# Threshold attention with a gated feed-forward on one core: v in longer packets, part of the threshold subtraction on GpSimd, and a planner that models shared transfer engines

## The chip, the core and the metric

The kernel runs on one core of a Trainium2 chip. The core has five engines with queues of their own: TensorE (PE, matrix products; PEld is its weight load), VectorE (DVE), ScalarE (ACT), GpSimd (POOL) and SyncE (SP, which here only issues DMAs). The metric is the device time of one execution in microseconds, lower is better; the time before is a median of three runs.

## The reference

```python
# q, k, v: (8, 8, 576, 64) float32; tau = 0.02; moe_w_in (512, 2048), moe_w_out (2048, 512) float64
scores = matmul(q, k.transpose(0, 1, 3, 2)) / sqrt(64)
thresh = max(scores, axis=-1) - tau                  # per query row
scores = where(scores >= thresh, scores, -1e9)
attn   = exp(scores - max(scores)) ; attn /= sum(attn, -1) + 1e-9
x      = matmul(attn, v)  -> (8*576, 512)            # heads side by side
h      = x @ w_in
out    = (h * sigmoid(1.702 * h)) @ w_out
```

Softmax sums, maxima and products with v do not depend on the order of the 576 keys, as long as k and v are taken in the same order.

## The kernel before

**Units of work.** The 64 heads are taken as 32 pairs (two heads of one batch entry, `n` = 0 to 31); four pairs make the 576 rows of one batch entry, and the feed-forward takes rows in blocks of 256. In a pair the 576 keys are nine chunks of 64 (`j`), the queries two halves. Scores lie transposed in SBUF, two chunks to a tile: four full tiles of 128x1152 and a tail of 128x576 (`t` = 0 to 4).

**The steps of a pair.** `load_qk` brings q and k with SP's queue (32x18x32 elements to a DMA, four each), `prep` (L477, DVE) transposes them, `scores_run` (L493, PE) makes a chunk of scores, `keep` (L510, ACT) copies it to SBUF, `in_groups` (L516, DVE) takes maxima tile by tile. `over_tiles`, `over_halves` and `turn_rows` make one row of thresholds, which goes to DRAM and back with `row_out` and `row_in` (SP) to be spread over the partitions (pair 2 spreads it with `spread_max` on DVE). Then for each of the five tiles: `sub` (L580, DVE) subtracts the threshold, `mask` (L586, ACT) and `exps` (L590, ACT) make the weights, and PE multiplies by v (`values`, L601, out `pv`). The sums come from PE for pairs 0 to 4 (`sums_by_pe`, L601, out `den`, read by `one_row`, L632), from `in_groups` again for the others: pairs 5 to 7 spread them with `one_group` and `spread_sums` on DVE, pairs 8 to 31 with `turn_sums`, `sums_out`, `sums_in` through DRAM. `place_x` (L703, DVE) multiplies `pv` by the reciprocal sums into `xT`. `load_v` brings v with four DMAs, 64x9x64 elements each (every key's 64 numbers are a run of 256 bytes).

**The weights.** `w_in` and `w_out` arrive as 64-bit numbers in 32 pieces (16 and 16). `load_w` (POOL's queue, two DMAs of about 512 KB a piece) brings one; `cv_ex`, `cv_frac` (two instructions), `cv_end` (L439, L453, L457, L465, DVE) and `cv_power` (L447, ACT) make float32 of it. Six staging places hold pieces in flight. `hold` (L484, POOL) keeps the first pieces back until the k of pairs 2 and 3 has been transposed.

**The feed-forward.** The first two blocks (`mm1_0`, L758, 128 products of 128x256; `mm2`, L740) wait for `place_x` of pairs 0 to 3 and for pieces of `w_in` in groups of four. Later blocks use `mm1` (L718) and `product` (L909), the last four blocks `product1` (L823).

**The order.** Nothing is ordered at run time: each engine's queue is written out by a planner (`run_in_order`), which simulates tasks with a cost, a lag and a rank each, and lets each engine take the ready task of the lowest rank. Ranks are the pair's number plus a table of biases by step (`EARLY` for pairs 0 to 3, `SECOND` for 4 to 7, `LATER`, and `CV` for weights). In the kernel before a load is one task with a fixed cost on its queue and a fixed lag until it has landed (9.0 for a weight piece, 3.0 to 10.0 for q and k). Engine queues run in order, so that an instruction that waits holds back all behind it.

Of the kernel before, what the change touches and what calls it, by code (L numbers as in the profile page):

```python
# [19 lines left out]
P = 128  # L20
# [10 lines left out]
def kernel(  # L31
# [84 lines left out]
    stop = const.tile([P, 1], FP32, name="stop")  # L116
    shift = const.tile([P, 1], FP32, name="shift")
# [9 lines left out]
    for x in ("raw0", "raw1", "qkT0", "qkT1", "mb"):  # L127
# [6 lines left out]
        "exps": -11.47,  # L134
        "in_groups": 5.75,
        "keep": 10.66,
        "load_qk": -0.27,
        "load_v": 4.86,
        "mask": -2.66,
        "one_group": -15.86,  # L140
        "one_row": 12.67,
        "over_halves": -7.01,
        "over_tiles": -4.01,
        "place_x": -17.11,
        "prep": -11.73,
        "row_in": 20.49,
        "row_out": 4.47,
        "scores_run": 12.45,
        "spread_max": -1.73,
        "spread_sums": 7.14,  # L150
        "sub": 9.27,
        "sums_by_pe": 0.27,
        "sums_in": -9.39,
        "sums_out": 2.13,
        "turn_rows": -12.55,
        "turn_sums": -0.41,
        "values": 14.64,
        "w_sum": 4.11,
        "x_sum": -14.1,
    }  # L160
    SECOND = {
        "exps": -7.29,
        "in_groups": 20.95,
        "keep": 16.67,
        "load_qk": -8.88,
        "load_v": 5.53,
        "mask": 2.36,
        "one_group": 2.55,
        "one_row": -2.71,
        "over_halves": -12.07,  # L170
        "over_tiles": 2.86,
        "place_x": -20.26,
        "prep": 3.49,
        "row_in": -19.42,
        "row_out": -24.08,
        "scores_run": -7.99,
        "spread_max": -3.11,
        "spread_sums": -2.29,
        "sub": 14.98,
        "sums_by_pe": 35.93,  # L180
        "sums_in": 7.43,
        "sums_out": 4.05,
        "turn_rows": -3.84,
        "turn_sums": 4.03,
        "values": 11.79,
        "w_sum": -10.45,
        "x_sum": -10.98,
    }
    LATER = {
        "exps": 2.01,  # L190
        "in_groups": 10.37,
        "keep": -0.02,
        "load_qk": -6.6,
        "load_v": 3.77,
        "mask": 14.79,
        "one_group": 4.78,
        "one_row": -14.98,
        "over_halves": 1.09,
        "over_tiles": -6.27,
        "place_x": -0.34,  # L200
        "prep": 2.34,
        "row_in": 4.02,
        "row_out": 2.64,
        "scores_run": -11.25,
        "spread_max": -9.44,
        "spread_sums": -6.73,
        "sub": 2.14,
        "sums_by_pe": 1.46,
        "sums_in": 3.78,
        "sums_out": 2.16,  # L210
        "turn_rows": 12.26,
        "turn_sums": 0.29,
        "values": -10.38,
        "w_sum": 6.61,
        "x_sum": 6.02,
    }
    CV = {
        "cv_end": -8.05,
        "cv_ex": 2.22,
        "cv_frac": -11.72,  # L220
        "cv_power": -4.72,
        "load_w": -7.79,
    }

    LAG = {"PE": 0.26, "DVE": 0.18, "ACT": 0.22, "POOL": 0.18}

    QUARTERS = ("scores", "scores_run", "values", "sums_by_pe")
# [12 lines left out]
    FIRST, LAST = -9.0, 1000.0  # L240
    need, follows = {}, {}

    def run_in_order():
# [7 lines left out]
        events = [(0.0, 1, i) for i, n in enumerate(left) if n == 0]  # L251
# [3 lines left out]
        mode, held_for = None, None  # L255
        while events:
            now = events[0][0]
            while events and events[0][0] <= now:
                _, kind, i = heapq.heappop(events)
                engine, _, rank, _, _, _, _, give, lag = tasks[i]  # L260
                if kind == 0:
                    busy.discard(engine)
                    heapq.heappush(events, (now + lag, 2, i))
                elif kind == 1:
                    ready.setdefault(engine, []).append((rank, i))
                else:
                    for pool in give:
                        free[pool] += 1

                for u in users[i]:  # L270
                    if kind == (0 if tasks[u][0] == engine else 2):
                        left[u] -= 1
                        if left[u] == 0:
                            ready.setdefault(tasks[u][0], []).append((tasks[u][2], u))
            for engine, queue in ready.items():
                if engine in busy:
                    continue
                for rank, i in sorted(queue):
# [14 lines left out]
                cost = tasks[i][1]  # L293
                if engine == "PE":
# [3 lines left out]
                heapq.heappush(events, (now + cost, 0, i))  # L298
                started += 1
# [4 lines left out]
    JOINT = 7  # L304

# [53 lines left out]
    def load_qk(n, which, queue):  # L359
# [4 lines left out]
        for h in range(2):  # L364
            for j in range(2):
                queue.dma_start(
                    out=blocks[ds(64 * h + 32 * j, 32), :, :],
                    in_=src[b, 2 * hp + h, :, ts(j, 32)].rearrange("(c p) d -> p c d", p=32),
# [3 lines left out]
    def load_v(n):  # L372
        b, hp = divmod(n, NPAIR)
        t = seat("v_m", n % 2).rearrange("p (j h d) -> p j h d", j=NK, h=2)
        for h in range(2):
            for c in range(2):
                nc.sync.dma_start(
                    out=t[ts(c, KT), :, h, :],
                    in_=v[b, 2 * hp + h].rearrange("(j k) d -> k j d", k=KT),
# [109 lines left out]
    def scores(n, j):  # L489
# [8 lines left out]
        if j == NK - 1:  # L498
# [33 lines left out]
    def over_halves(n):  # L532
        r = stats[n, ALU.max]
        o = work.tile([P, QB], FP32, name="fold", tag="fold", bufs=1)
        for x in (1, 3) if n in BY_DMA else range(4):
# [3 lines left out]
            )  # L539
        if n in BY_DMA:  # L540
# [10 lines left out]
    def turn_rows(n):  # L551

        nc.vector.transpose(out=flat[1], in_=flat[0])

# [23 lines left out]
    def sub(n, t):  # L578
        s = sT[n, t].rearrange("p u h s -> p u (h s)")
        nc.vector.tensor_tensor(  # L580
# [26 lines left out]
    def values(n, tiles):  # L607
# [3 lines left out]
        by_values(n, lambda j, h: v_m[:, j, h, :], [pv[:, c, :] for c in range(2)], tiles)  # L611
        if n < NPAIR:
            free_scores(n, tiles)

    def sums_by_pe(n, tiles, apart):
# [9 lines left out]
        if not apart:  # L625
# [321 lines left out]
    nc.gpsimd.memset(ones, 1.0)  # L947
    nc.gpsimd.dma_start(
# [26 lines left out]
    BY_PE = 5  # L975
    BY_DMA = (0, 1, *range(3, NP))
    SUMS_BY_DMA = range(8, NP)
    LEAD = 6
    WHOLE = 6

    FFU = 1.727
    T_RANK = FIRST

    W_RANK = (0, 12.87, 12.51, 22.24, 0, 4.97)
    ready_w, w_loads, w64 = [], [], 0
    for i in range(len(pieces)):
# [10 lines left out]
        a = task("POOL", 1.1, rank, load_w, i, after=w_loads[-1:], take=place, lag=9.0)  # L997
        w_loads.append(a)
        e = task("DVE", 0.345, rank, cv_ex, i, after=[a])
        m = task("ACT", 0.67, rank, cv_power, i, after=[e])  # L1000
        a = task("DVE", 1.1, rank, cv_frac, i, after=[e])

        over = [ready_w[y] for y in range(i) if i >= n_in and stage(y) == (i - n_in) // PER_STAGE]
        ready_w.append(task("DVE", 0.61, rank, cv_end, i, after=[a, m] + over, give=place))
# [191 lines left out]
    for n in range(NP):  # L1196
# [5 lines left out]
        slow = 1.1 if n < NPAIR else 1.0  # L1202
# [3 lines left out]
        cost = 3.5 if NPAIR <= n < 2 * NPAIR else 2.0  # L1206
        lag = (4.6, 3.0)[n] if n < 2 else 10.0 if n < 2 * NPAIR else 3.0
        lq = task("SP", cost, r - 2.0, load_qk, n, 0, q0, after=behind, take=own(n, "raw0"), lag=lag)
        lk = task(
            "SP", cost if n else 0.1, r - 2.0, load_qk, n, 1, q1, after=behind,  # L1210
            take=own(n, "raw1"), lag=lag,
        )
        v_m = f"v_m{n % 2}"
        lv = task("SP", 2.4, r + (1.85 if n < 2 else -1.2), load_v, n, after=lvs[-1:], take=(v_m,), lag=3.0)
        lvs.append(lv)
        pq = task("DVE", 0.69, r, prep, n, 0, after=[lq], take=own(n, "qkT0"), give=own(n, "raw0"))
# [45 lines left out]
        else:  # L1262
            for js in [range(x, x + 3) for x in range(0, NK, 3)] if n >= WHOLE else [[x] for x in range(NK)]:
# [4 lines left out]
                    give=own(n, "qkT0", "qkT1") if js[-1] == NK - 1 else (),  # L1268
# [4 lines left out]
        a = task("DVE", 0.35, r, over_tiles, n, ALU.max, after=mx)  # L1273
        a = task(
            "DVE", 0.8 if n in BY_DMA else 1.05, r, over_halves, n, after=[a, tau_done],
# [100 lines left out]
```

## Time and profile before

| | |
|---|---|
| median of three runs | 1317.71 us (1317.33 to 1318.2) |
| profiled execution: time, span | 1317.94 us, 1316.2 us |
| mean granted TensorE clock | 0.987 |
| busy: PE, DVE, ACT, POOL | 1260.9, 1006.1, 646.6, 249.0 us |
| first matmul of the feed-forward (`mm1_0`) | 117.60 us after the span's start |

The profiled execution lasts 1.74 us longer than its span. PE's busy time and its idle time add up to the span, so that the kernel's time can be read as PE's work plus the gaps in PE's queue. Idle time of another engine counts only where it turns into such a gap.

### The profile page before, as it was taken

Reading aid. Unit: us, or ns where it says so; the run is one execution under the profiler, and the core shown is the slowest. Engines: PE = TensorE matmul, PEld = TensorE weight load, DVE = VectorE, ACT = ScalarE, POOL = GpSimd, SP = SyncE. Lnnn points to the kernel's source line nnn. Section 1 sums busy time; section 2 is a strip of 40 time slices with the busy share of each in tenths; the row PEclk is TensorE's granted clock in tenths of the full one; section 3 lists DMA queues with packets and bytes.
Section 4 is the critical chain, followed back from the end, with each engine's and each line's share of the span. In section 5 each row is a group of like instructions: output and inputs, shape, how many; then the busy total and the mean of one; then the engine's idle time right before and its main releaser. Section 6 shows DMA issues by size and latency. Waiting matters only on the chain. (4 is left out here: it accounts for less than half of the span.)

```text
span 1316.2 us, 22807 instructions
## 1 busy us (share of the span) xinstructions
PE 1260.9 (96%) x9128; PEld 975.6 (74%) x9128; DVE 1006.1 (76%) x1610; ACT 646.6 (49%) x830; POOL 249.0 (19%) x291
## 2 busy tenths in 40 slices
PE   5669999999999999999999999999999999999998
PEld 2346864457887777777778888777777778888887
DVE  7989999898888887788777877777888863652642
ACT  4876666576554555555554555454556540210210
POOL 1201211012031211213021303030212117120120
PEclk8879999999999999999999999999999999999999
DMA  8976766545323223212213222323122110000000
GB/s 152 293 189 207 230 207 149 112 77 100 85 55 71 55 55 71 51 50 54 58 42 72 55 71 55 71 55 71 36 55 54 36 46 8 9 1 25 8 0 32
DMA packets 258819, 102.88 MB, mean 78 GB/s; under 512 B 233754, under 2 KB 243994, under 8 KB 258714
## 3 DMA queue, kind: packets, MB, share of 16 engines
q1 hardware_dynamic: 244986, 63.40, 22.4%
q0 software_dynamic: 11360, 37.74, 9.3%
q8 instruction: 71, 1.16, 0.4%
q10 hardware_dynamic: 2368, 0.30, 0.2%
q14 instruction: 34, 0.28, 0.1%
HBM read 87.51 MB, written 9.69 MB: 74 GB/s over the span
## 5 line engine op out<-in xcount | busy, mean ns | idle before, releaser
L516 DVE TRANSPOSE_TENSOR_REDUCE part<-arena 128x36 f32<-128x1152 f32 (+1 forms) x295 | 357.5, 1235 | 41.9 <-ACT arena L510 32.4
L718 PE MATMUL hps<-xT,w_in 128*128 128x256 f32 x1536 | 337.2, 380 | 0.5 <-DVE arena L730 0.4
L718 PEld LDWEIGHTS hps<-xT,w_in 128*128 128x128 f32 x1536 | 290.7, 190 | 45.9 <-issue 5.7
L586 ACT ACTIVATE arena<-arena 128x1152 f32<-128x1152 f32 (+1 forms) x160 | 169.4, 1059 | 144.0 <-DVE arena L580 143.8
L510 ACT COPY arena<-ps 128x576 f32<-128x576 f32 x288 | 170.7, 647 | 115.3 <-PE ps L493 111.9
L580 DVE TENSOR_TENSOR arena<-arena 128x1152 f32<-128x1152 f32 (+1 forms) x158 | 201.1, 1313 | 20.5 <-DMA arena<-row 20.5
L909 PE MATMUL ops<-w_out,arena 128*128 128x256 f32 x896 | 202.4, 380 | 1.8 <-DVE arena L730 1.8
L590 ACT ACTIVATE arena<-arena,shift,scl 128x1152 f32<-128x1152 f32 (+1 forms) x160 | 200.3, 1252 | 4.1
L493 PE MATMUL ps<-arena 64*64 64x288 f32 x2304 | 174.7, 420 | 22.9 <-DVE arena L477 15.3
L909 PEld LDWEIGHTS ops<-w_out,arena 128*128 128x128 f32 x896 | 169.3, 190 | 28.7 <-DVE arena L730 3.1
L875 POOL TENSOR_TENSOR arena<-arena 128x256 f32<-128x256 f32 x56 | 49.7, 888 | 647.1 <-DVE arena L730 543.9
L601 PE MATMUL pv<-arena 64*64 64x288 f32 x2176 | 159.7, 408 | 0.0
L727 ACT ACTIVATE th<-hps 128x512 f32<-128x512 f32 x112 | 66.0, 589 | 186.0 <-PE hps L718 171.8
L909 PE MATMUL ops<-arena 128*128 128x256 f32 x672 | 150.7, 380 | 0.7 <-DVE osb L931 0.7
L493 PEld LDWEIGHTS ps<-arena 64*64 64x64 f32 x2304 | 84.0, 137 | 90.8 <-ACT arena L510 30.4
L909 PEld LDWEIGHTS ops<-arena 128*128 128x128 f32 x672 | 127.1, 190 | 20.4 <-issue 2.2
L601 PEld LDWEIGHTS pv<-arena 64*64 64x64 f32 x2176 | 82.1, 134 | 54.1 <-issue 10.0
L931 DVE SCALAR_TENSOR_TENSOR osb<-ops,osb 128x256 f32<-128x256 f32 x98 | 39.3, 413 | 97.9 <-PE ops L909 90.6
L730 DVE SCALAR_TENSOR_TENSOR arena<-th,hps 128x512 f32<-128x512 f32 x96 | 64.2, 669 | 46.7 <-ACT th L727 46.4
L740 PE MATMUL ops<-w_out,arena 128*128 128x512 f32 x128 | 57.2, 600 | 3.2 <-DVE w_out L465 2.2
L758 PE MATMUL hps<-xT,w_in 128*128 128x256 f32 x256 | 56.4, 381 | 0.0
L888 POOL TENSOR_TENSOR arena<-arena 128x512 f32<-128x512 f32 x28 | 35.6, 1272 | 108.3 <-PE ops L909 108.3
(115 smaller groups left out, 1044.7 us busy)
## 6 DMA issues: line engine op xcount, KB each, us to landing
arena<-in_v_dram SPq DMA_DIRECT2D x128, 144.0 KB
arena<-in_q_dram SPq DMA_DIRECT2D x128, 72.0 KB
out_dram<-osb SPq DMA_DIRECT2D x36, 256.0 KB
arena<-in_k_dram SPq DMA_DIRECT2D x124, 72.0 KB
arena<-row SPq DMA_DIRECT2D x62, 144.0 KB
arena<-row_s SPq DMA_DIRECT2D x48, 144.0 KB
w_out<-in_moe_w_in_dram POOLq DMA_DIRECT2D x12, 512.0 KB, 9.5
arena<-in_moe_w_out_dram POOLq DMA_DIRECT2D x12, 512.0 KB, 6.3
```

The lines of the kernel that those rows point to most:

```text
L493: nc.tensor.matmul(ps[ts(c, KT), h, 0:SH], lhsT=mats[n, 1][ts(h, D), ts(j, KT)], rhs=mats[n, 0][ts(h, D), ts(c, SH)], start=True, stop=True,)
L510: nc.scalar.copy(out=sT[n, t][:, u], in_=pss.pop((n, j))[:, :, 0:SH])
L516: nc.vector.tensor_reduce(out=stats[n, op][:, t * 2 * QB : min(2 * t + 2, NK) * QB], in_=sT[n, t].rearrange("p u h (g d) -> p (u h g) d", ...
L580: nc.vector.tensor_tensor(out=s, in0=s, in1=mbs[n].unsqueeze(1).to_broadcast(list(s.shape)), op=ALU.subtract)
L586: nc.scalar.activation(out=s, in_=s, func=AF.Prelu, alpha=STEEP)
L590: nc.scalar.activation(out=s, in_=s, func=AF.Exp, scale=scl, bias=shift)
L601: nc.tensor.matmul(o[c][ts(h, D), 0:SH], lhsT=left(j, h)[ts(c, KT)], rhs=sT[n, t][ts(c, KT), u, h, :], start=(j == 0), stop=(j == NK - 1),)
L718: nc.tensor.matmul(hidden[j][:, ts(f, BLK)], lhsT=w_in[:, c, ds((f * HF + j) * P, P)], rhs=xTs[blk][:, c, :], start=(c == 0), stop=(c == N ...
L727: nc.scalar.activation(out=ths[j], in_=hidden[j], func=AF.Tanh, scale=GELU_SCALE / 2)
L730: nc.vector.scalar_tensor_tensor(out=g[:, :, j, :], in0=two(ths.pop(j)), scalar=1.0, in1=two(hidden.pop(j)), op0=ALU.add, op1=ALU.mult,)
L740: nc.tensor.matmul(acc[i], lhsT=g0[:, j, ts(i, P)], rhs=w_out[:, j, :], start=(j == 0), stop=(j == NFC - 1),)
L909: nc.tensor.matmul(banks[blk][k][:, ts(o, HM)], lhsT=left[:, j, :], rhs=right[:, j, :], start=(j == 0), stop=(j == HF - 1),)
```

## The change

It has five parts:

1. `load_v` reads nine keys in a row for each partition (`(k j) d` for `(j k) d`): one run of 2304 bytes instead of nine of 256. For the keys to agree, `load_qk` reads k in the same order, with the same runs of 128 bytes.
2. `sub` of tiles 1, 3 and 4 (two full ones and the tail) is issued on GpSimd for pairs 0 to 7.
3. The sums of pairs 5 to 7 go through DRAM too (`SUMS_BY_DMA = range(5, NP)`).
4. The planner gets two more queues, "DMS" for SP's transfers and "DMW" for the weights'. A load is an issue and a transfer; two transfers at a time share the engines, SP's with a share of 0.055 (q, k, rows out) or 0.3 (v, rows in). Several costs change, and `cv_frac` and `cv_end` get 0.2 us each for sharing with GpSimd.
5. All bias tables have new numbers, so that every queue is in another order up to about pair 8; from there on PE's order is the same.

`TWICE` is empty, so that `row_blocks`, `again` and `mask_one` are never called; but the constants for them (`minus`, `own_row`) are set up on GpSimd at the start, ahead of the load of `tau`.

```diff
+    minus = const.tile([P, 2, KT], FP32, name="minus")
+    own_row = const.tile([P, QB // 2], FP32, name="own_row")
...
     EARLY = {
-        "exps": -11.47,
-        "in_groups": 5.75,
-        "keep": 10.66,
-        "load_qk": -0.27,
+        "exps": -8.59,
+        "in_groups": 25.1,
+        "keep": -15.3,
+        "load_qk": 26.17,
...
+    SHARE = (0.055, 0.3)
+
+    def transfer(by, time, a, kind=0, give=(), lag=1.7):
+        return task(by, time, FIRST, moved, kind, after=[a], give=give, lag=lag)
...
+        def rates():
+            if len(flow) < 2:
+                return dict.fromkeys(flow, 1.0)
+            x = SHARE[tasks[flow["DMS"][0]][4][0]]
+            return {"DMS": x, "DMW": 1.0 - x}
...
+    TWICE = ()
+    BY_POOL = dict.fromkeys(range(8), (1, 3, 4))
...
+                rows = src[b, 2 * hp + h, :, ts(j, 32)]
                 queue.dma_start(
                     out=blocks[ds(64 * h + 32 * j, 32), :, :],
-                    in_=src[b, 2 * hp + h, :, ts(j, 32)].rearrange("(c p) d -> p c d", p=32),
+                    in_=rows.rearrange("(a p t) d -> p t a d", a=2, p=32) if which
+                    else rows.rearrange("(c p) d -> p c d", p=32),
                 )
...
-        t = seat("v_m", n % 2).rearrange("p (j h d) -> p j h d", j=NK, h=2)
+        t = seat("v_m", n % 2).rearrange("p (h j d) -> p h j d", j=NK, h=2)
         for h in range(2):
             for c in range(2):
                 nc.sync.dma_start(
-                    out=t[ts(c, KT), :, h, :],
-                    in_=v[b, 2 * hp + h].rearrange("(j k) d -> k j d", k=KT),
+                    out=t[ts(c, KT), h],
+                    in_=v[b, 2 * hp + h].rearrange("(k j) d -> k j d", k=KT),
                 )
...
-        nc.vector.tensor_tensor(
+        engine = nc.gpsimd if t in BY_POOL.get(n, ()) else nc.vector
+        engine.tensor_tensor(
             out=s, in0=s, in1=mbs[n].unsqueeze(1).to_broadcast(list(s.shape)), op=ALU.subtract
         )
...
+    nc.gpsimd.memset(minus, 0.0)
+    nc.gpsimd.memset(own_row, 0.0)
+    for x in range(4):
+        nc.gpsimd.memset(minus[ts(x, 32), x % 2, :], -1.0)
+        nc.gpsimd.affine_select(
+            out=own_row[ts(x, 32)], in_=own_row[ts(x, 32)], compare_op=ALU.not_equal, fill=1.0,
+            base=-(QB // 2) * (x // 2), pattern=[[-1, QB // 2]], channel_multiplier=1,
+        )
...
-    BY_PE = 5
+    SUMS_BY_PE = (0, 1, 2, 3, 4)
     BY_DMA = (0, 1, *range(3, NP))
-    SUMS_BY_DMA = range(8, NP)
+    SUMS_BY_DMA = range(5, NP)
...
-        a = task("POOL", 1.1, rank, load_w, i, after=w_loads[-1:], take=place, lag=9.0)
+        a = task("POOL", 1.1, rank, load_w, i, after=w_loads[-1:], take=place)
         w_loads.append(a)
-        e = task("DVE", 0.345, rank, cv_ex, i, after=[a])
+        a = transfer("DMW", 3.4, a)
+        e = task("DVE", 0.42, rank, cv_ex, i, after=[a])
...
+            pool = t in BY_POOL.get(n, ())
             a = task(
-                "DVE", 0.67 if tail else 1.35, r, sub, n, t, after=subs[-1:],
+                "POOL" if pool else "DVE", (1.45 if pool else 0.67) if tail else 2.7 if pool else 1.35,
+                r, sub, n, t, after=[y for y, x in subs if tail or x in (None, pool)],
                 give=own(n, "mb") if tail else (),
             )
```

## The prediction

> **What bounds the kernel now.** First the page: busy times and the span in 40 slices of 32.9 us.
>
> ```profile
> PE 1260.9 (96%) x9128; PEld 975.6 (74%) x9128; DVE 1006.1 (76%) x1610; ACT 646.6 (49%) x830; POOL 249.0 (19%) x291
> ...
> PE   5669999999999999999999999999999999999998
> ...
> DVE  7989999898888887788777877777888863652642
> ACT  4876666576554555555554555454556540210210
> ```
>
> PE is busy for 1260.9 of 1316.2 us; 55.3 us is the most that any reordering can win at these matmul times. The gaps are in the first four slices, where DVE stands at 7, 9, 8, 9 and ACT at 4 to 8: there PE is fed, later it is the bound. Next PE's timeline over the start (start, length, engine, line; in brackets the idle time before and who ended it).
>
> ```profile
> 8.29 11.57 PE L493 MATMUL ps<-arena 64*64 64x288 f32 x144 [8.29 <-DVE arena L477]
> 25.97 5.84 PE L493 MATMUL ps<-arena 64*64 64x288 f32 x64 [6.11 <-DVE arena L477]
> ...
> 38.77 2.20 PE L601 MATMUL den<-arena,ones 64*64 64x288 f32 x16 [6.96 <-DVE w_out L457]
> ...
> 81.58 7.59 PE L601 MATMUL den<-arena,ones 64*64 64x288 f32 x72 [10.82 <-DVE r L632]
> ...
> 117.60 1.99 PE L758 MATMUL hps<-xT,w_in 128*128 128x256 f32 x8
> ```
>
> The feed-forward begins at 117.60 us and does not pause for 60 us. By the windows PE is idle for 41 us until then, always behind DVE or ACT, for 3.4 after its last matmul, and for 11 in between. Where the gaps are the granted clock falls too (0.63 to 0.85 in windows of ten): den x72 at 81.58 took 7.59 us, against 4.54 for the same 72 at 164.50. What sets 117.60? ACT, DVE and SP:
>
> ```profile
> 36.13 1.16 ACT L586 ACTIVATE arena<-arena 128x1152 f32<-128x1152 f32 x1 [3.46 <-DVE arena L580]
> ...
> 89.96 1.16 ACT L586 ACTIVATE arena<-arena 128x1152 f32<-128x1152 f32 x1 [4.37 <-DVE arena L580]
> ...
> 100.42 0.87 ACT L590 ACTIVATE arena<-arena,shift,scl 128x576 f32<-128x576 f32 x1
> ```
>
> ```profile
> 88.56 2.63 DVE L580 TENSOR_TENSOR arena<-arena 128x1152 f32<-128x1152 f32 x2 [3.70 <-DMA arena<-row]
> ...
> 114.40 0.95 DVE L703 TENSOR_TENSOR xT<-pv,arena 128x256 f32<-128x256 f32 x4
> ```
>
> ```profile
> 51.66 22.87 SPq L377 DMA_DIRECT2D arena<-in_v_dram  x8
> ...
> 82.19 0.71 SPq L566 DMA_DIRECT2D row<-flat  x2
> 84.86 1.12 SPq L575 DMA_DIRECT2D arena<-row  x2
> ```
>
> ACT works from 36.13 to 101.19 on masks and exponentials of pairs 0 to 3 with 9.4 us idle, 4.37 of it because DVE waited 3.70 us for pair 3's row of thresholds. That row was turned at 77.85 but left SP only at 82.19, behind v of pairs 2 and 3 (51.66) and q and k of pair 4. After 101.19, PE's order still has scores of pairs 4 and 5 ahead of pair 3's last products; `place_x` of pair 3 runs at 114.40.
>
> **Parts 1 and 4, ACT's order.** I counted the instructions of both orders and priced them by step, start to start in the timelines: mask 1.18, exp 1.26 (tail 0.70, 0.78), keep 0.59, cv_power 0.68 us. Four pairs of mask and exp are 4 x (4 x 2.44 + 1.48) = 45.0. Before, ten keeps (5.9) and seven cv_power (4.8) lie among them, and 9.4 idle: 65.1, the trace's stretch. After, 22 keeps (13.0) and eight cv_power (5.4): 63.4. So the scores that came after pair 3's exponentials are now mixed among them, and from the same start (36.1: DVE must first finish the maxima of pairs 0 to 2, unchanged, until 34.4) ACT alone would end at 99.5. Pair 3's column sums and `place_x` follow (0.84 + 0.18 + 0.27 + 0.78 + 0.95, and about 1 for PE): 103.5. Idle time must be added. Gone: the 4.37, since v of nine keys is 256 packets for a pair instead of 2304 and SP's order puts pair 4's q and k ahead of pair 3's v. Staying: waits of 0.3 to 1.2 us on PE and DVE (4.7 in all before, of which I keep 2), and a new one: POOL's queue issues pieces 6 to 11 between pair 3's first subtraction and its other two. Six pieces took from 26.01 to 37.76 on that queue (waits for landings included), 6.5 without waits. ACT has 9.7 us of other work there, so the wait is 0 to 5 us; I take 1.5. Feed-forward start: 103.5 + 3.5 = 107.
>
> **Part 2, subtraction on GpSimd.** DVE loses 8 x (2 x 1.28 + 0.67) = 25.8 us. On POOL no such shape is in the trace; the nearest rows:
>
> ```profile
> 290.10 0.73 POOL L875 TENSOR_TENSOR arena<-arena 128x256 f32<-128x256 f32 x1 [5.36 <-DVE arena L730]
> ...
> 305.66 1.76 POOL L875 TENSOR_TENSOR arena<-arena 128x256 f32<-128x256 f32 x1 [7.29 <-DVE arena L730]
> ...
> 336.25 1.28 POOL L888 TENSOR_TENSOR arena<-arena 128x512 f32<-128x512 f32 x1 [13.28 <-PE ops L909]
> ...
> 1095.37 1.71 POOL L797 TENSOR_TENSOR arena<-w_in 128x512 f32<-128x512 f32 x1
> ```
>
> 256 columns take 0.73 and 512 take 1.28 us alone, 2.15 ns a column more: 1152 would take 2.66, 576 1.42, a pair 6.7, under ACT's 11.2 us for the pair, so POOL's pace is covered if its queue is free. But beside DVE it is slower, and so is DVE:
>
> ```profile
> 1088.52 0.69 DVE L797 TENSOR_TENSOR arena<-w_in 128x512 f32<-128x512 f32 x1
> ...
> 1090.26 1.21 DVE L806 TENSOR_TENSOR arena<-xT 128x512 f32<-128x512 f32 x1
> 1094.80 1.16 DVE L806 TENSOR_TENSOR arena<-xT,arena 128x512 f32<-128x512 f32 x1
> ```
>
> A DVE tensor_tensor of 512 columns took 0.69 alone and 1.16 to 1.21 beside POOL's line 797 (1.71 instead of 1.28): DVE loses 0.42 of the shared time. In the head, DVE's eight remaining subtractions (10.2) and the arithmetic of eight weight pieces (16.1) are 0.44 of the 60.3 us it still has to do. Per subtraction on POOL (mean 2.25, stretched by a third to 3.0) that is 3.0 x 0.44 x 0.42 = 0.55 us; 24 of them 13 us. Ends: 0 (at 305.48 two DVE subtractions took 2.55 as always, and POOL's 256 columns 1.76: POOL paid alone) and 2.25 (DVE stands for a whole one). I take 0.55, from the rows with sustained overlap of both. The Trainium skill, "SBUF — State Buffer", section "Who interferes with whom", speaks against the change: a VectorE instruction with two SBUF inputs and a GpSimd instruction that reads SBUF exclude each other, and the later one blocks until the first is done. The row at 305.66 looks like that; the sustained rows show both running at part speed. By the full rule DVE would wait about half a subtraction, 1.1 us each, 27 us for 24, and the 25.8 us would be gone.
>
> DVE's sum to `place_x` of pair 3, by the same kind of count: before 100.1 us, after 86.5. The difference: subtractions -12.9, eight weight pieces instead of 12.7 -9.4, maxima of pairs 4 and 5 pulled forward +7.0 and their row +1.6. After the maxima of pair 2 (26.2 of the sum, at 34.4) 60.3 remain; with 12 x 0.55 that is 101.3, plus 3 for DMA waits 104.3. ACT's 107 ends later and is taken. Gain: 117.6 - 107, and 0.5 because the chunk of scores that follows the first products of `mm1_0` before is now ahead of it: 11 us.
>
> **After the start: parts 2, 3 and deferred pieces.** From there until `place_x` of pair 8 DVE had 174.2 us of work and PE 175.3, with 6.8 idle. After: DVE 157.5 + 6.6 = 164.1 (five more pieces, 12 fewer subtractions, maxima done earlier; part 3 saves about 1.2 for each of three pairs), PE 168.3 (16 `mm1` of 0.44 moved behind). PE's margin over DVE grows from 1.1 to 4.2, so idle falls by about 2, and by 6.8 at most. Part 3's two transfers have room: the sums come after `exps`, and pairs 8 on show 1.1 us of waiting for such a row in all. Behind pair 8 PE's order is equal: nothing. The new constants on POOL delay `tau` at 1.39 by ten small instructions (0.1 to 0.3 each by the memsets) and perhaps 0.68 of set-up (POOL's configuration step at 284.1); it landed 3.9 later and is used at 9.16, so 0 to 1 us, covered by PE's first nine chunks. k's new order keeps size and number of its runs: 0, either way no more than the 0.1 us between the issue of four q (2.17) and four k (2.06).
>
> Sum, against the profiled execution: 1317.9 - 11 - 2 = 1305. The median lies 0.2 under that execution, which I leave.
>
> **Rivals.** (a) Contention eats the gain: at 1.08 us per subtraction (25.8 / 24) DVE gains nothing. At 1.0 the head gives 107 + 5.4 = 112.4, a gain of 5.7, and in the second phase DVE's 169.5 exceeds PE's 168.3, idle 1 to 5 worse: 1313 to 1317. For it: both engines read the same kind of tiles all the time. Against: 0.56 of DVE's stream in the head is neither kind (maxima, transposes, sums). (b) Slower: DVE is stopped for nearly the whole of each subtraction, 2 us. Head: 34.4 + 60.3 + 24 + 3 = 121.7, start at 122.5, 5 later than now; second phase 157.5 + 24 = 181.5 against 168.3 of PE, idle 13 instead of 6.8: +6, in all 1329; from 1.08 us on it begins to lose (1320 to 1332). Against it: no DVE row grew by more than 1.1. (c) More than summed: ACT never idles (start 103.5) and the second phase has no gaps: 1317.9 - 14.5 - 6.8 = 1297, and a few less if the clock stays up. (d) The change does not do what it says, weight DMAs on POOL's queue hold the subtractions: up to 5 us of the head, 1310; it lies inside my case.
>
> **How the numbers follow.** My case (1298 to 1312) 0.60; (a) 0.14, of it 0.06 faster, 0.06 same, 0.02 slower; (b) 0.17; (c) 0.09 (1294 to 1298). What can be told from no change is 0.2%, 2.6 us. Faster 0.75, same 0.06, slower 0.19. The range 1295 to 1320 leaves out most of (b) and half of (c).
>
> **What would show it.** Right: first `mm1_0` at 104 to 111; no SP stretch of 20 us at v; the subtraction on POOL 2.7 to 3.5 us; DVE's weight steps (0.69) grown to 0.8 to 1.0 in the head; PE idle about 42 us. Wrong: DVE rows beside POOL at 2 us or more; ACT waiting for POOL by more than 5 us before the start; new PE gaps between 110 and 290 of more than 10 us.

## The result, and the profile after

The changed kernel took 1362.46 us (median of 4, 1357.19 to 1368.52) against 1317.95 before: ratio 1.033, interval 1.0273 to 1.0386. It is slower by 44.5 us; the forecast was 1305, range 1295 to 1320. The profiled execution took 1365.45 us, span 1363.7.

The page's busy times and the slices, which answer to the four lines of before (each slice is now 34.1 us):

```profile
PE 1266.4 (93%) x9128; PEld 978.9 (72%) x9128; DVE 1022.9 (75%) x1577; ACT 640.4 (47%) x830; POOL 309.9 (23%) x325
...
PE   4287797979999999999999999999999999999998
...
DVE  4899899988988777778777887778787874562642
ACT  4397545666655554445445555555454550110210
```

PE is busy for 5.5 us more at the same count of matmuls, and idle for 97.3 us instead of 55.3. The second slice (34.1 to 68.2 us) holds a 2 for PE and a 3 for ACT, where before held 6 and 8. DVE, which feeds both, has a 4 in the first slice, where it had a 7.

PE's timeline over the start and a little beyond (start, length, engine, line, operation; in brackets the idle time before and who ended it):

```profile
10.13 12.14 PE L538 MATMUL ps<-arena 64*64 64x288 f32 x144 [10.13 <-DVE neg L1054]
...
60.80 4.12 PE L687 MATMUL den<-arena,ones 64*64 64x288 f32 x32 [33.33 <-ACT arena L676]
...
131.61 14.08 PE L844 MATMUL hps<-xT,w_in 128*128 128x256 f32 x64
153.36 16.78 PE L844 MATMUL hps<-xT,w_in 128*128 128x256 f32 x64 [7.67 <-DVE arena L850]
...
284.80 1.24 PE L538 MATMUL ps<-arena 64*64 64x288 f32 x8 [9.05 <-ACT arena L555]
```

The feed-forward starts at 131.61, not 117.60. One gap of 33.33 us ends at 60.80. After the start, where before PE hardly paused, there are gaps of 7.67 and 9.05 us. Busy time by windows gives PE's idle time in three stretches:

| kernel (profiled execution) | 0 to 120 | 120 to 300 | 300 to the end | all |
|---|---|---|---|---|
| before | 41.0 | 6.8 | 7.5 | 55.3 |
| after | 52.5 | 33.3 | 11.5 | 97.3 |

Split at the first feed-forward matmul instead, the idle time is 57.5 and 39.8 us, where before had 41.0 and 14.3. So the larger part of the new idle time lies behind the stretch on which the forecast worked hardest. Two things show at the first gap. The first is in the queues of SP (the first fence is the kernel before) and DVE:

```profile
23.50 0.86 SPq L566 DMA_DIRECT2D row<-flat  x2
26.20 1.13 SPq L575 DMA_DIRECT2D arena<-row  x2
```

```profile
9.13 5.13 SPq L422 DMA_DIRECT2D arena<-in_v_dram  x8
...
22.76 2.68 SPq L410 DMA_DIRECT2D arena<-in_k_dram  x4
25.54 2.27 SPq L651 DMA_DIRECT2D row<-flat  x2
37.06 1.14 SPq L660 DMA_DIRECT2D arena<-row  x2
```

```profile
37.43 0.78 DVE L522 STREAM_TRANSPOSE arena<-arena 128x576 f32<-128x576 f32 x1 [10.72 <-DMA arena<-in_k_dram]
```

In the changed kernel v of pairs 0 and 1 (8 DMAs from 9.13) goes ahead of q and k of pairs 2 and 3. k of pair 3 is issued from 22.76 on, while POOL's queue issues three weight pieces from 23.61, and k lands so late that DVE stands for 10.72 us. The row of pair 0 (4.4 KB) is issued at 25.54, and SP can send it back only at 37.06; before, the two steps stood at 23.50 and 26.20. ACT's first mask, at 36.13 before, runs at 44.67.

The second is DVE beside POOL's three subtractions:

```profile
42.00 6.56 POOL L666 TENSOR_TENSOR arena<-arena 128x1152 f32<-128x1152 f32 x3
```

```profile
44.67 1.16 ACT L672 ACTIVATE arena<-arena 128x1152 f32<-128x1152 f32 x1 [16.34 <-POOL arena L666]
```

```profile
41.77 1.37 DVE L561 TRANSPOSE_TENSOR_REDUCE part<-arena 128x36 f32<-128x1152 f32 x1
43.18 5.68 DVE L581 TENSOR_SCALAR fold<-red,gap 32x18 f32<-32x18 f32 x2
48.90 0.49 DVE L594 SCALAR_TENSOR_TENSOR flat<-red,gap,fold 32x18 f32<-32x18 f32 x2
49.42 0.21 DVE L605 STREAM_TRANSPOSE flat<-flat 128x32 f32<-128x32 f32 x1
49.55 3.86 DVE L561 TRANSPOSE_TENSOR_REDUCE part<-arena 128x36 f32<-128x1152 f32 x3
```

POOL subtracts from 42.00 to 48.56; ACT had waited 16.34 us for the first of the three. Two `tensor_scalar` of 32x18 (line 581; the two steps of the same size at 48.90 take 0.49) take 5.68 us. Taken singly, the first is 5.42 us of it and ends when GpSimd is through with all three. The maximum at 41.77, which runs into the first subtraction, keeps its length; those at 49.55 start behind the last. The gap of 7.67 us at 153.36 is of the same kind: one step of a weight piece, beside POOL's subtractions from 148.10 to 152.08, takes 5.25 us, and the gelu that PE waits for stands behind it on DVE:

```profile
147.12 5.25 DVE L484 TENSOR_SCALAR w_out<-w_out 128x512 uint32<-128x512 uint32 x1
152.29 0.41 DVE L484 TENSOR_SCALAR arena<-arena 128x512 uint32<-128x512 uint32 x1
152.63 0.67 DVE L850 SCALAR_TENSOR_TENSOR arena<-th,hps 128x512 f32<-128x512 f32 x1
```

### The profile page after: what moved, and what is told of

It is laid out like the page before. It is cut to its first block, busy times and chain, and to the rows that moved or that the text cites. A ratio compares the mean times of both kernels' runs of the same rounds, so it can differ in the third digit from the quotient of the medians.

```text
span 1363.7 us, 22848 instructions
## 1 busy us (share of the span) xinstructions
PE 1266.4 (93%) x9128; PEld 978.9 (72%) x9128; DVE 1022.9 (75%) x1577; ACT 640.4 (47%) x830; POOL 309.9 (23%) x325
## 3 DMA queue, kind: packets, MB, share of 16 engines
q8 instruction: 71, 1.16, 0.4%
## 4 chain that ended last, share of the span: by engine, by line
PE 70%; DVE 4%; ACT 2%; DMA 2%; SPq 1%; issue 0%; POOL 0%; DVEq 0%
PE ops L995 25%; PE hps L804 21%; PE pv L687 7%; PE ps L538 7%; PE ps L909 4%; PE ps L995 4%; PE ops L909 3%; DVE part L561 1%; ACT arena L676 1%; ACT arena L672 1%; DVE arena L666 1%; DMA arena<-in_k_dram 1%; DMA arena<-row 1%; ACT arena L555 1%; DMA row_s<-flat_s 0%
## 5 line engine op out<-in xcount | busy, mean ns | idle before, releaser
L804 PE MATMUL hps<-xT,w_in 128*128 128x256 f32 x1536 | 340.5, 382 | 3.7 <-DVE arena L816 3.7
L672 ACT ACTIVATE arena<-arena 128x1152 f32<-128x1152 f32 (+1 forms) x160 | 164.5, 1059 | 195.5 <-DVE arena L666 172.5
L666 DVE TENSOR_TENSOR arena<-arena 128x1152 f32<-128x1152 f32 (+1 forms) x136 | 193.8, 1465 | 18.1 <-DMA arena<-row 18.1
L676 ACT ACTIVATE arena<-arena,shift,scl 128x1152 f32<-128x1152 f32 (+1 forms) x160 | 194.4, 1245 | 1.1
L687 PEld LDWEIGHTS pv<-arena 64*64 64x64 f32 x2176 | 82.2, 135 | 55.3 <-issue 11.7
L687 PE MATMUL den<-arena,ones 64*64 64x288 f32 x360 | 29.8, 463 | 44.1 <-ACT arena L676 44.1
L666 POOL TENSOR_TENSOR arena<-arena 128x1152 f32<-128x1152 f32 (+1 forms) x22 | 57.7, 2649 | 54.9 <-DMA arena<-row 36.6
L844 PE MATMUL hps<-xT,w_in 128*128 128x256 f32 x256 | 59.6, 394 | 7.7 <-DVE arena L850 7.7
```

The costliest lines, as they stand in the source:

```text
L666: engine.tensor_tensor(out=s, in0=s, in1=mbs[n].unsqueeze(1).to_broadcast(list(s.shape)), op=ALU.subtract)
L672: nc.scalar.activation(out=s, in_=s, func=AF.Prelu, alpha=STEEP)
L676: nc.scalar.activation(out=s, in_=s, func=AF.Exp, scale=scl, bias=shift)
L687: nc.tensor.matmul(o[c][ts(h, D), 0:SH], lhsT=left(j, h)[ts(c, KT)], rhs=sT[n, t][ts(c, KT), u, h, :], start=(j == 0), stop=(j == NK - 1),)
L804: nc.tensor.matmul(hidden[j][:, ts(f, BLK)], lhsT=w_in[:, c, ds((f * HF + j) * P, P)], rhs=xTs[blk][:, c, :], start=(c == 0), stop=(c == N ...
```

## The experiments

Theory 1: DVE is stopped for nearly the whole of each GpSimd subtraction (the forecast's rival (b)). Theory 2: the new order places small transfers (k, rows) beside large ones, and these waits make the loss. Differences in us below are against the median of the runs of before on the same chip (1317.1 to 1320.2).

**1. v and k alone.** The kernel before with `load_v` and `load_qk` of the change; plan and subtractions stay.

```
-    in_=v[b, 2 * hp + h].rearrange("(j k) d -> k j d", k=KT),
+    in_=v[b, 2 * hp + h].rearrange("(k j) d -> k j d", k=KT),
```

> The kernel before with the first part alone: keys reordered, v in packets of nine keys, the old plan and all subtractions on VectorE. Neither theory says that this part lost the time. Both expect the v transfers of 20 us on SP's queue to fall to about 3 us each and the first FFN matmul to stay within 5 us of the old 117.6 us: 1308 to 1318 us. If this part were behind the loss, the time would be over 1325.

1320.91 us, ratio 1.002 (1.0002 to 1.0038): 3 us above the expected range, but below the 1325 from which on this part would be behind the loss. SP's queue in the kernel before and in this run, each in two windows (50 to 58 and 58 to 76 us), and PE's in this run:

```profile
51.66 3.87 SPq L377 DMA_DIRECT2D arena<-in_v_dram  x4
66.77 7.76 SPq L377 DMA_DIRECT2D arena<-in_v_dram  x4
```

```profile
54.81 2.54 SPq L379 DMA_DIRECT2D arena<-in_v_dram  x4
69.92 2.46 SPq L379 DMA_DIRECT2D arena<-in_v_dram  x4
```

```profile
69.25 0.66 PE L603 MATMUL pv<-arena 64*64 64x288 f32 x8
```

The stretch of 22.87 us that the forecast laid on v's packets (51.66 in before) is two loads of four DMAs with a wait of some 11 us between. v of pair 3 waits for its buffer until pair 1's products are through, here at 69.91. The loads take 2.54 and 2.46 us, in the kernel before 3.87 and 7.76. Nearly all that they save (6.6 us) is lost by the loads behind them on the queue: four DMAs of q take 8.44 us instead of 5.35, four of k 5.12 instead of 2.12. The wait for pair 3's row, which the forecast wanted to win with this part, is still 4.04 us, at 92.07.

**2. The lock out.** The changed kernel, its order kept, all subtractions on VectorE.

```
-        engine = nc.gpsimd if t in BY_POOL.get(n, ()) else nc.vector
+        engine = nc.vector
```

> The changed kernel, its order on every other queue kept, but the three subtractions of a pair that GpSimd took are issued on VectorE at the same place of the order. Theory 1 (VectorE is stopped for nearly the whole of each GpSimd subtraction): the excess of about 40 us on VectorE's rows goes (the reduce of 32x18 beside GpSimd back from a mean of 517 ns to 261, the weight step out of 866 to 420) and 24 subtractions of 1.3 and 0.7 us come back, some 26 us; net a gain, 1330 to 1348 us, with first FFN matmul at 120 to 130. Theory 2 (the loss is the late k of pair 3 behind the weight pieces, and the order of the new plan): VectorE gets 26 us of work more, nothing else changes, and the time is 1355 to 1375.

1354.03 us, ratio 1.027 (1.0222 to 1.0317): neither theory's number, nearest to theory 2's, and 8 us below the changed kernel. The trace says why so little came back: with DVE free, a later collision turned up.

```profile
36.71 0.78 DVE L522 STREAM_TRANSPOSE arena<-arena 128x576 f32<-128x576 f32 x1 [10.26 <-DMA arena<-in_k_dram]
...
121.46 0.78 DVE L522 STREAM_TRANSPOSE arena<-arena 128x576 f32<-128x576 f32 x1 [15.21 <-DMA arena<-in_k_dram]
```

k of pair 3 is as late as before the edit (10.26). k of pair 4 was issued from 97.43 to 101.41; from 99.13 to 109.68 POOL's queue issued six weight pieces, and DVE waited for that k for 15.21 us.

**3. The lock in.** The mirror: the kernel before, its plan and its loads, tiles 1, 3 and 4 of pairs 0 to 7 subtracted by GpSimd at DVE's places.

```
-        nc.vector.tensor_tensor(
+        engine = nc.gpsimd if n < 8 and t in (1, 3, 4) else nc.vector
+        engine.tensor_tensor(
```

> The kernel before, its plan and its v loads, with one edit: tiles 1, 3 and 4 of pairs 0 to 7 are subtracted on GpSimd, at the places where VectorE did it. Theory 1: VectorE is rid of 26 us of subtractions and stopped for some 55 us (24 GpSimd subtractions of 2.6 and 1.4 us) whenever it has work: 1330 to 1355 us. Theory 2: the old plan has no late k, so moving the subtractions alone costs at most their longer latency: 1305 to 1322.

1334.35 us, ratio 1.0115 (1.0074 to 1.0155), 17 us over before: theory 1's number.

**4. Weights held.** Experiment 2, planned with all first six weight pieces behind pair 3's k.

```
-            for a in w_loads[3 * (n - 2) : 3 * (n - 1)]:
+            for a in w_loads[: 6 if n == 3 else 0]:
```

> The second experiment (subtractions on VectorE) with a plan in which all first six weight pieces wait for pair 3's k, where the changed kernel let three go at pair 2's k. Theory 2: k of pair 3 and the row of pair 0 no longer share the queues with weight packets; VectorE's wait of 10.7 us at 27 to 37 us goes, and the time falls by 8 to 14 us below the second experiment's. Theory 1 alone: within 4 us of the second experiment, since VectorE's work after the head sets the end.

1345.50 us, ratio 1.0202 (1.0173 to 1.023), 8.5 below experiment 2: theory 2's number. DVE's wait for pair 3's k is 0.95 us. But the edit goes through the planner, and the traces show that it moved steps in the queues of VectorE, ScalarE and TensorE as well, so that the 8.5 us are not the weights' alone. Yet the kernel stands 28 us above before, with nothing on GpSimd and an early k.

**5. Weights held, the lock back in.** As the changed kernel, with only the edit of experiment 4.

> The changed kernel with all first six weight pieces held behind pair 3's k, and the subtractions on GpSimd as the change has them: the fourth experiment with the lock back in. Theory 1 (VectorE stopped beside GpSimd's subtractions) expects it 10 to 20 us above the 1345.5 us of that experiment, since the old order paid 17 us for the same: 1355 to 1366. Theory 2 (the new order's transfers alone make the loss) expects it within 5 us of 1345.5. Against the changed kernel's 1362.5 it shows what the early release of three weight pieces cost while VectorE was stopped as well.

1360.18 us, ratio 1.0318 (1.0292 to 1.0343), 14.7 over experiment 4 (13.4 when each is taken against its own runs of before): theory 1's number. The orders of TensorE, ScalarE and SP are those of experiment 4, so this pair shows the stops alone. Against the changed kernel it is only 2.3 lower, within the spread of that kernel's four runs. With DVE stopped, then, no gain of an earlier k can be told; that the two causes hide each other fits this, but the 8.5 and the 2.3 us are too close to the spread to show it.

**6. Subtractions nobody uses.** The kernel before, whose DVE keeps all its work; GpSimd subtracts on a spare tile at the same places.

```
...
+        if n < 8 and t in (1, 3, 4):
+            for _ in range(s.shape[1]):
+                nc.gpsimd.tensor_tensor(out=dump, in0=dump, in1=mbs[n][:, 0:512], op=ALU.subtract)
```

> The kernel before, VectorE keeps all its subtractions, and GpSimd does subtractions that nobody uses (two of 128x512 for a tile of two scores, one for the last tile, on a spare tile) at the places of tiles 1, 3 and 4 of pairs 0 to 7. No work waits for them, so longer latency can't cost anything. Theory 1: the stops of VectorE alone, with no relief of 26 us beside them: some 45 us of GpSimd's busy time, most of it beside VectorE's work: 1335 to 1360 us. If the 17 us of the third experiment were the longer latency of a GpSimd subtraction and not a stopped VectorE: 1315 to 1322.

1343.32 us, ratio 1.0194 (1.0161 to 1.0227), 25 us over before. No work waits for these results, so the stops alone, without any latency, can make a loss of experiment 3's size.

**7. The relief alone.** As experiment 3, but GpSimd subtracts one column.

```
+            nc.gpsimd.tensor_tensor(
+                out=s[:, :, 0:1], in0=s[:, :, 0:1], in1=..., op=ALU.subtract)
+            return
```

> The kernel before with the subtractions of tiles 1, 3 and 4 of pairs 0 to 7 left out but for one column, which GpSimd does at VectorE's place (that part of the threshold subtraction is left out of the result). VectorE is rid of 26 us, the waits and the order stay as in the third experiment, nothing is stopped for long. It is the most that the move could give if GpSimd cost VectorE nothing. Theory 1: 1300 to 1312 us, as the forecast's relief of some 12 us said, so the third experiment's stops cost some 20 to 30 us in all. Rival: VectorE's relief is not on the path, and the time is 1314 to 1320, so that the stops cost 17 us alone.

1315.47 us, ratio 0.9976 (0.9955 to 0.9998): the rival's number. 26 us less work on VectorE bring 3. The busy lines of this run and of experiment 3, which differ only in the width of the GpSimd subtraction:

```profile
PE 1258.4 (96%) x9128; PEld 974.4 (74%) x9128; DVE 983.2 (75%) x1586; ACT 645.9 (49%) x830; POOL 256.7 (20%) x315
```

```profile
PE 1265.7 (95%) x9128; PEld 977.4 (73%) x9128; DVE 1011.7 (76%) x1586; ACT 646.7 (48%) x830; POOL 310.3 (23%) x315
```

DVE's busy time is 983.2 against 1011.7 for the same instructions: 28.5 us of stops, 1.19 per subtraction, and the time differs by 19.

**8. The kinds of instruction.** 

> No part of the computation: nine kinds of VectorE's instructions, four of each alone and then twelve beside three GpSimd subtractions of 128x1152 back to back. Theory 1: those kinds that the changed kernel's trace shows stretched (the small and the 128x512 tensor_scalar, tensor_tensor, scalar_tensor_tensor) stop until GpSimd is through, up to 8 us for one; reduces and transposes run at their usual length. Rival (shared by turns): all kinds run at up to twice their length and none stops for over 2 us.

The first row shows three of a kind alone, the others twelve of a kind beside three GpSimd subtractions, which took 7.98 to 9.25 us together:

```profile
16.16 1.53 DVE L96 TENSOR_SCALAR dst<-src,one 128x512 f32<-128x512 f32 x3
...
17.72 12.90 DVE L96 TENSOR_SCALAR dst<-src,one 128x512 f32<-128x512 f32 x12
...
70.42 10.23 DVE L112 SCALAR_TENSOR_TENSOR red<-src,one 32x18 f32<-32x18 f32 x12
...
83.70 9.37 DVE L118 SCALAR_TENSOR_TENSOR dst<-src,one,ps 128x512 f32<-128x512 f32 x12
...
121.58 16.93 DVE L131 TRANSPOSE_TENSOR_REDUCE red<-src 128x36 f32<-128x1152 f32 x12
```

`tensor_scalar` of 128x512 (line 96) takes 0.51 us alone; twelve would be 6.1 us and take 12.90. By the same sum the 32x18 `scalar_tensor_tensor` (70.42) loses 7.2 us, the 32x18 `tensor_scalar` 7.2, `tensor_tensor` of 128x576 and `scalar_tensor_tensor` of 128x512 about 6.8 each: nearly GpSimd's whole run. Here the two engines take turns: taken singly, three of the twelve are held, each through one subtraction (2.71 us instead of 0.48 at 18.24). The `scalar_tensor_tensor` with one input in PSUM (83.70), the transpose, the transposing reduce (121.58) and the plain reduce lose some 0.1 us in twelve. This is theory 1, with its list of kinds.

**9 and 10. The sum transfers.** What loses 28 us in experiment 4? Its PE gaps behind the start, and what SP, POOL and DVE do at the second:

```profile
113.36 1.56 PE L844 MATMUL hps<-xT,w_in 128*128 128x256 f32 x6 [1.76 <-DVE r L718]
...
255.18 1.24 PE L538 MATMUL ps<-arena 64*64 64x288 f32 x8 [7.82 <-DVE xT L789]
...
315.75 1.24 PE L538 MATMUL ps<-arena 64*64 64x288 f32 x8 [8.49 <-ACT arena L555]
```

```profile
299.94 1.54 POOL L955 DMA_DIRECT2D arena<-w_out  x1 [55.66 <-ACT arena L951]
```

```profile
303.80 3.01 SPq L660 DMA_DIRECT2D arena<-row  x2
```

```profile
312.62 5.16 DVE L666 TENSOR_TENSOR arena<-arena 128x1152 f32<-128x1152 f32 x4 [9.49 <-DMA arena<-row]
```

The head is now better than before's (113.36 against 117.60 for the first feed-forward matmul). But a transfer of 1 MB that adds weight blocks (`t_plus`, issued at 299.94) lies on the row trip of 303.80, DVE waits for the row for 9.49 us, ACT behind it, and PE for 8.49. Both kernels were run with these four transfers cut to one column, the new order (on top of experiment 4) and the old:

```
-        o, a, _ = T_SUMS[x]
+        o, a, _ = (y[:, 0:1, 0:1] for y in T_SUMS[x])
```

> The fourth experiment (new order, weights held, subtractions on VectorE) with the four transfers of 1 MB that add weight blocks on chip cut to one column each (that part of the weight sums is left out). What is open is where its 27 us over the kernel before lie, when nothing stops VectorE and pair 3's k is early. Its trace shows a row trip of 9.5 us and one of 4.9 us that TensorE waits for, beside such transfers. Theory 2a (the order puts small row trips beside large transfers): the two gaps of 8 us fall below 3 and the time is 1330 to 1338. Rival (order of engines alone, the trips are incidental): 1342 to 1347.

> The same cut in the kernel before, the control for the run beside it: there the row trips near these transfers cost VectorE 3.6 us once and TensorE nothing over 2 us. Theory 2a: 1313 to 1318. If the transfers bear on both orders alike, the time falls here by as much as there.

New order 1334.45 us (ratio to before 1.011, 1.0091 to 1.013), old order 1313.98 (0.9966, 0.9953 to 0.9979). The gaps of 7.82 and 8.49 fall to 2.06 and 2.84. The old order gains 6 us too. Of the 28 us between the orders 20.5 remain, so these collisions made 8.

**11 and 12. No large transfers.** Experiment 2 and the kernel before, with the weight pieces cut to 64 bytes a row too (the buffers are filled with zeros at the start).

```
-        nc.gpsimd.dma_start(out=t.rearrange("p c w -> p (c w)"), in_=dram.bitcast(U32))
+        nc.gpsimd.dma_start(out=t.rearrange("p c w -> p (c w)")[:, 0:16], in_=dram.bitcast(U32)[:, 0:16])
...
```

> The second experiment (new order and its release of weights, subtractions on VectorE) with every weight piece cut to the first 64 bytes of a row and the sums to one column, after a fill of the buffers at the start (the weights are left out of the result). No large transfer is left beside q, k and the rows but v and the output. Theory 2 (the new order loses by transfers that starve small ones): the waits of 10 and 15 us for k go, and the time is 1318 to 1330. Rival (the engine order itself is worse, whatever the transfers do): 1340 to 1352.

> The same cut and fill in the kernel before, the control: its order has the weights behind pair 3's k, so little should change: VectorE's waits for rows (7.5 us up to 300 us) shrink, 1306 to 1317. The distance from the run beside it is then what the order costs without large transfers: under 14 us by theory 2, over 25 us by its rival.

New order 1323.28 us (1.0025, 1.0015 to 1.0036), old order 1308.79 (0.9917, 0.9899 to 0.9936). The distance between the orders falls from 37 us (experiment 2) to 14.5, half a us over what theory 2 allowed: 22.5 us went with the large transfers. VectorE's waits for k in the first 300 us fall from 26.3 us in experiment 2 to 1.2. The rest is not in the head, where the new order's feed-forward now starts at 111.68 against 113.00. From 120 to 300 us PE is idle for 15.7 us in the new order and 4.8 in the old, and the longest gap there is one behind ACT:

```profile
248.72 1.24 PE L540 MATMUL ps<-arena 64*64 64x288 f32 x8 [7.32 <-ACT arena L557]
```

```profile
244.34 3.81 ACT L678 ACTIVATE arena<-arena,shift,scl 128x1152 f32<-128x1152 f32 x3
248.05 0.61 ACT L557 COPY arena<-ps 128x576 f32<-128x576 f32 x1
```

The copy that frees PSUM (line 557) stands in ACT's order behind three exponentials, and PE waits for 7.32 us.

**13 and 14. The old rank tables.** Is this rest in the new tables of rank offsets (theory 2b)? The new planner with the old tables, on top of experiments 11 and 2.

> The new planner without large packets and with the subtractions on VectorE, as in the run that stood 14.5 us over its control, but with the old tables of rank offsets (the numbers by kind of work that set who goes first) in place of the new ones. Theory 2b (the rest of the loss is the new tables' order: copies that free PSUM behind exps, pair 0's subtractions behind the maxima of the next pairs): within 6 us of the control's 1308.8. Rival (the new planner's prices and transfer model make the order worse whatever the tables): 1318 to 1330.

> The second experiment (new order, subtractions on VectorE, all transfers whole) with the old tables of rank offsets. Theory 2b: below the second experiment's 1354 by 14 us or more, 1325 to 1340; the rest above 1318 would be the weight release ahead of pair 3's k. Rival: 1345 to 1360.

1351.06 us (1.0238, 1.0208 to 1.0267) and 1368.33 (1.0369, 1.0344 to 1.0394): both above theory 2b's numbers and above the rival's. The old tables do worse with the new prices than the new ones do, and they do it in the head: the feed-forward starts at 147.84 and 157.90. Behind it PE is idle for only 15.0 and 20.0 us, with the new tables (experiments 11 and 2) for 23.7 and 31.4, in the old order's run (experiment 12) for 12.1. Whether the old tables leave less idle time there, or only the later start does, is not separated, and what makes the last 14.5 us stays open beyond the gap just named.

**15. Sums on VectorE.** A complete kernel: before, with the four weight-block sums as one VectorE subtraction each.

```
-        nc.gpsimd.dma_start(out=o, in_=a, accum_op=ALU.add)
+        nc.vector.tensor_tensor(out=o, in0=a, in1=b, op=ALU.subtract)
```

> The kernel before, complete, with the four weight-block sums of 1 MB made by VectorE (one subtraction of 128x2048 each, some 2.3 us by twice the row of 128x1152) in place of ScalarE's eight negations and GpSimd's four adding transfers. The runs with these transfers cut to a column were 4 to 6 us faster, and 26 us less work on VectorE brought 3 us, so 9 us more should cost 1 to 2: 1313 to 1318, against 1318 before. If VectorE's queue is in the way at those four places (a wait for TensorE in front of other work), 1318 to 1324.

1320.07 us, ratio 1.0003 (0.9989 to 1.0017): no gain, and in the range expected if VectorE's queue is in the way. The four take 2.25 us each, as expected, and a PE gap of 2.52 us behind VectorE at 287.93 is new; what gives the rest of the expected gain back is not separated. No complete kernel of the study is faster than the one before.

## Why the prediction was wrong

| | GpSimd subtracts | VectorE subtracts |
|---|---|---|
| old order | 1334.4 (experiment 3) | 1318 (before) |
| new order, weights held | 1360.2 (experiment 5) | 1345.5 (experiment 4) |
| new order, as changed | 1362.5 (the changed kernel) | 1354.0 (experiment 2) |

Each run taken against the runs of before on its own chip, reading across gives the price of the stops, less the relief: 17, 13 and 8 us from top to bottom. Reading down gives the price of the new order: 25 and 28 us with the weights held, 27 and 37 as the change has it. Either way the order is the larger part of the 44.5. What the early release of three weight pieces costs by itself is not separated, as the planner moved other steps with it. The forecast had the first at a small loss inside a gain, and the second as the gain itself.

**The subtraction's price, 0.55 us.** This term failed. The forecast worked from the rows at 1088 to 1095, where VectorE lost 0.42 of the shared time, and set them above the rule of the Trainium skill, "SBUF — State Buffer", section "Who interferes with whom". The rule was right: for the kinds it names (two SBUF inputs, `tensor_scalar`), VectorE stands until GpSimd is through (5.42 us instead of 0.23 at 43.18). The rows that looked like part speed also fit engines that take turns, as in experiment 8, and the same window of before has a longer one, which the forecast's 1.16 to 1.21 leaves out:

```profile
1092.53 1.75 DVE L806 TENSOR_TENSOR xT<-xT 128x512 f32<-128x512 f32 x1
```

The runs add two things that made it dearer than the 1.1 us the forecast reckoned by it. A VectorE instruction can be held through several GpSimd subtractions in a row, and the smallest are held too: the forecast's share of 0.44 (subtractions and weight steps) left out the steps of 32x18 that make a row of thresholds (0.23 us each). VectorE's busy time is 1019.8 in experiment 5 and 1003.3 in experiment 4, which does 25.8 us more on it: 42.3 us of stops for 24 subtractions, 1.76 each, near the 2 of rival (b). In the old order it was 1.19.

**The break-even of 1.08 us.** It compared sums: 24 stops against 25.8 us of relief. In the old order the sums almost meet (28.5 against 25.8), yet 17 us were lost. Experiment 7 shows one half of why: the relief is worth 3 us, so VectorE's subtractions at those places were hardly what PE waited for. The other half, that the stops fall on steps that the next mask or piece of weights waits for, is a reading of rows like 43.18 and 147.12, not shown by a run of its own. Two equal sums on one engine are not worth the same time.

**"From the same start (36.1)".** The step "maxima of pairs 0 to 2, unchanged, until 34.4" failed: k of pair 3 reached VectorE at 37.43 and pair 0's row came back late. The forecast counted the instructions ahead on each queue, and SP's queue is shorter, but not what else the transfer engines would move: three weight pieces are released by pair 2's k, and v's eight DMAs pushed pair 3's k into them. ACT started at 44.67, 8.6 us late. The greater failure of the head is the 3.5 us of idle time that the forecast added to ACT's 63.4 us of work. With just the instructions that it counted (20 masks, 20 exponentials, 22 keeps, 8 powers), ACT took 82.3 us to 127.00, and 20.2 of them were idle: 7.5 behind VectorE's subtractions, 6.6 behind VectorE's weight steps (beside GpSimd 2.83 and 2.85 us instead of 0.42), 3.0 behind PE, and 2.6 behind GpSimd, whose queue issued six weight pieces ahead of its second subtraction for pair 3 (the forecast's 1.5). Where neither cause is in (experiment 4), the feed-forward starts at 113.36: the new head was worth 4 us there, not 11.

**The 4.37 us of the late row.** The forecast laid SP's 22.87 us on v's 2304 packets; about half of them are a wait for pair 1's buffer (experiment 1). Without large transfers 2304 packets were as quick: in experiment 12 the two loads take 2.70 and 2.67 us. It was right that the changed kernel has no such stretch (four v DMAs take 2.4 to 4.1 us up to 420 us). The wait is gone because v of pair 3 now stands behind q and k of pair 4.

**After the start, -2 us.** PE's idle time from 120 to 300 rose from 6.8 to 33.3 us. The forecast compared work (164.1 against 168.3) and let the difference be idle time. Experiments 4, 9 and 11 show single waits of this kind, rows behind 1 MB transfers and copies behind exponentials, in stretches with work to spare.

**Right:** a GpSimd subtraction of 1152 and 576 columns takes 2.63 and 1.40 us alone (2.66 and 1.42 forecast); ACT's wait for POOL and VectorE rows of 2 us and more were named as signs that would prove the forecast wrong, and both are there (16.34 and 5.42 us); the third sign, a new PE gap of over 10 us from 110 to 290, is not (the longest is 9.05). **Rival (b)** had the mechanism and 1329 us: it kept the gain of the order, and so missed by 33. **Rival (a)** adds VectorE's 5.4 us to ScalarE's 107; by the forecast's own rule the later of 107 and 104.3 + 5.4 = 109.7 counts, so its head is 2.7 too long. TensorE's start went from 8.29 to 10.13, released by the terms of `tau`, whose load left POOL at 2.85 instead of 1.39; the forecast had this covered by PE's first chunks.

## What to carry to other kernels

Before work goes to GpSimd, list what VectorE does beside it by kind: here steps with two SBUF inputs and `tensor_scalar` steps stopped, reduces, transposes and a step with one input in PSUM ran on; and price a stop by the whole run of GpSimd instructions, not by one. When an order is rebuilt, look at each small transfer that somebody waits for (k, a row of 4 KB) and ask which large ones are in the queues between its issue and its landing: in this case the large transfers made 22.5 of the 37 us between the orders, more than the stops. And ask what a relief is worth before its price: moving the work away for free (one column instead of 1152) takes one run.

## What the runs showed of the hardware

- Three GpSimd subtractions in a row can hold one VectorE instruction through all three: 5.42 us for a step of 0.23 (43.18 in the changed kernel), 7.83 for one of 1.3 (208.78). In experiment 8 the engines took turns instead; the sum lost there was nearly the same, GpSimd's whole run.
- Small transfers land late beside large ones of another queue: a row of 4.4 KB needed some 11 us from its issue to SP's next step beside weight pieces (25.54 to 37.06), 2.7 before; four DMAs of k about 20 us beside six pieces (experiment 2). Without large transfers VectorE's waits for k all but vanish (experiment 11).
- Idle time of PE and the length of its matmuls have no simple rule here: with 85.9 us idle (experiment 5) the same matmuls were busy for 1273.0 us at a mean granted clock of 0.972, with 103.6 idle (experiment 14) for 1260.5 at 0.970, before, with 55.3 idle, for 1260.9 at 0.987.
